# Second half of the first token chunk transposed by DMA instead of on TensorE, one PSUM bank per strip of the first half, and the small GELU and gate parameters loaded from ScalarE's queue

## The chip, the cores and the metric

The kernel runs on one core of a Trainium2 chip. The metric is the device time of one execution in microseconds (us). The profile's times count from the start of its span, which is about 1.8 us shorter than the device time of the same execution (218.6 against 220.37 us in the profiled run of the kernel before). The engines are called PE (TensorE; PEld is its weight load), ACT (ScalarE), DVE (VectorE), POOL (GpSimd) and SP (SyncE, which here only issues DMAs). "SPq" and "ACTq" in a trace line mean the queue of that engine while it issues a DMA.

## The reference, cut to what matters

Two branches over the same 2048 tokens of width 640 are mixed by a gate. Branch A is a state-space model: a complex linear recurrence along the tokens between two projections. Branch B is an MLP, 640 to 1728 to 640, with GELU.

```python
x = A_x                                                   # (1, 2048, 640) bf16
g = _sigmoid((x * gate_w).sum(-1, keepdims=True))
a = _A_ref(x, A_Lambda_re, ..., A_log_dt, A_Dskip)        # h = Lam_bar*h + x@B_bar ; y = 2*Re(h@C) + x*D
b = _B_ref(x, B_w1, B_b1, B_w2, B_b2)                     # gelu(x@w1 + b1) @ w2 + b2
return g * a + (1 - g) * b
```

## The kernel before

The tokens go in four chunks of 512. The first matmuls of both branches (x@w1, x@B_bar) sum over the features of a token and here read them along the partitions, so every chunk is needed transposed (`xT`). Chunks 1 to 3 come transposed by DMA. Chunk 0 is on the path to the first useful matmul, so it is loaded as it lies, in two halves of 256 tokens, and transposed on TensorE; VectorE and ScalarE copy the result from PSUM. The first matmuls are FF1 (x@w1) of chunk 0: six output tiles held in six PSUM banks, first for the first token half, then for the second. Tiles 7 to 14 follow; then the state-space stage ("SSM", first weights `BT_re`), and from there PE runs without a break to the end.

```python
    load_xn(0, 0, H)                                     # first 256 tokens, as they lie (SP queue)
    nc.scalar.dma_start(out=prmA[0:KS, :], in_=A_log_dt...)      # three small loads, ACT queue
    ...
    for kd in range(KD):                                 # KD = 5
        nc.sync.dma_start(out=w1a[kd][:], in_=B_w1[kd * P:(kd + 1) * P, 0:cut1])    # tiles 1 to 6
    load_xn(0, H, TPC)                                   # second 256 tokens
    for kd in range(KD):
        nc.sync.dma_start(out=w1b[kd][:, 0:F - cut1], in_=B_w1[..., cut1:F])        # tiles 7 to 14
    ...
    nc.gpsimd.dma_start(out=prmB[...], in_=B_b1...)      # three small loads, POOL queue: b1, gate_w
    nc.sync.dma_start_transpose(out=BT_re[:], in_=A_B_re[:, :])
    ...
    pA = bank(BF16)                                      # 8 PSUM banks in all
    pT = bank(BF16)

    def strip(kd, h):                                    # four strips in one bank, the fifth in pA
        return pT[:, kd * HT:(kd + 1) * HT] if kd < 4 else pA[:, (h + 1) * HT:(h + 2) * HT]

    def transposes(h):                                   # ten PE transposes of 128x128
        ...
    def take(kd, h):
        dst = xT[0][:, kd, h * HT:(h + 1) * HT]
        if kd % 2 == 0:
            nc.vector.tensor_copy(out=dst, in_=strip(kd, h))
        else:
            nc.scalar.activation(out=dst, in_=strip(kd, h), func=ACT.Identity)
    ...
    banks = [bank() for _ in range(FA)]                  # FA = 6
    for kd in range(KD):
        if kd == KD - 1:                                 # second token half, before the last kd of the first
            transposes(1)
            for j in range(KD):
                take(j, 1)
        for kf in range(FA):
            ff1_mm(banks[kf], 0, kf, kd, 0, HT)
    nc.scalar.activation(out=FS[:, :, 0:HC], in_=red, func=ACT.Sin, scale=TWO_PI_M)   # SSM's rotation tables
    ...                                                  # more Sin, then:
    for kd in range(KD):
        for kf in range(FA):
            ff1_mm(banks[kf], 0, kf, kd, HT, CH)         # second token half
        if kd == 2:
            nc.tensor.transpose(pA[:, P:P + NB], prmB[:], ident[0:NB, 0:NB])          # b1, gate_w to columns
            ...
    for kf in range(FA):
        ff1_act(banks[kf], 0, kf)                        # GELU: frees the six banks
    ff1(0, FA)                                           # tiles 7 to 14
```

Of the kernel before, what the change touches and what calls it, by code (L numbers as in the profile page):

```python
# [11 lines left out]
ACT = mybir.ActivationFunctionType  # L12
BF16 = mybir.dt.bfloat16
# [3 lines left out]
P = 128  # L17
T = 2048
D = 640
F = 1728  # L20
CH = 512
NCH = T // CH
KD = D // P
KS = D // P
KF = (F + P - 1) // P
F_LAST = F - (KF - 1) * P
NT = T // P
TPC = CH // P
# [10 lines left out]
def kernel(  # L39
# [19 lines left out]
    nc = tc.nc  # L59
    x2d = A_x.flatten_outer_dims()  # L60
# [11 lines left out]
    def bank(dtype=F32):  # L72
        return ps.tile([P, CH * 4 // (4 if dtype == F32 else 2)], dtype, name="bank")
# [4 lines left out]
    xT = [const.tile([P, KD, CH], BF16, name=f"xT{c}") for c in range(NCH)]  # L78
# [9 lines left out]
    ident = const.tile([P, P], BF16, name="ident")  # L88
    prmA = const.tile([3 * KS, P], BF16, name="prmA")
    NB = KS + KF  # L90
    prmB = const.tile([NB, P], BF16, name="prmB")
# [10 lines left out]
    xn = [None] * NCH  # L102
# [7 lines left out]
    H = TPC // 2  # L110

    def load_xn(c, a0=0, a1=TPC):
        if a0 == 0:
            xn[c] = xnp.tile([P, TPC, D], BF16, name="xn")
        r0 = c * CH + a0 * P
        nc.sync.dma_start(out=xn[c][:, a0:a1, :], in_=x2d[r0:r0 + (a1 - a0) * P, :].rearrange("(a p) d -> p a d", p=P))
# [4 lines left out]
    nc.scalar.dma_start(out=prmA[2 * KS:3 * KS, :], in_=A_Lambda_re.rearrange("(j p) -> j p", p=P))  # L121
    for kd in range(KD):
        nc.sync.dma_start(out=w1a[kd][:], in_=B_w1[kd * P:(kd + 1) * P, 0:cut1])
    load_xn(0, H, TPC)
    for kd in range(KD):
        nc.sync.dma_start(out=w1b[kd][:, 0:F - cut1], in_=B_w1[kd * P:(kd + 1) * P, cut1:F])
    make_identity(nc, ident[:])
    HC = CH // 4
    tfi = work.tile([P, HC], I32, name="e")
    nc.gpsimd.iota(tfi[:], pattern=[[1, HC]], base=0, channel_multiplier=0)  # L130
    nc.gpsimd.memset(prmB[:], 0.0)
    nc.gpsimd.dma_start(out=prmB[KS:NB - 1, :], in_=B_b1[0:(KF - 1) * P].rearrange("(j p) -> j p", p=P))
    nc.gpsimd.dma_start(out=prmB[NB - 1:NB, 0:F_LAST], in_=B_b1[(KF - 1) * P:F].rearrange("(j p) -> j p", p=F_LAST))
    nc.gpsimd.dma_start(out=prmB[0:KS, :], in_=gate_w.rearrange("(j p) -> j p", p=P))
    nc.sync.dma_start_transpose(out=BT_re[:], in_=A_B_re[:, :])
    nc.sync.dma_start_transpose(out=BT_im[:], in_=A_B_im[:, :])
    nc.sync.dma_start_transpose(out=xT[1][:], in_=x2d[CH:2 * CH, :])
# [5 lines left out]
    nc.sync.dma_start(out=Dbc[:], in_=A_Dskip.rearrange("(o d) -> o d", o=1).to_broadcast([P, D]))  # L143
    nc.sync.dma_start_transpose(out=xT[2][:], in_=x2d[2 * CH:3 * CH, :])
    nc.sync.dma_start_transpose(out=xT[3][:], in_=x2d[3 * CH:4 * CH, :])
    load_xn(1)

    ctx.enter_context(tc.manual_schedule(engines={E.PE, E.DVE, E.Activation}))


    class Clock:
        pe = 5.2
        act = 13.0
        dve = 0.0

# [36 lines left out]
    for _ in range(2):  # L192
        nc.tensor.matmul(wps[:, 0:P], lhsT=warm[:, 0:P], rhs=warm[:, 0:P], start=True, stop=True)
    pA = bank(BF16)
    pT = bank(BF16)
    HT = H * P


    def strip(kd, h):
        return pT[:, kd * HT:(kd + 1) * HT] if kd < 4 else pA[:, (h + 1) * HT:(h + 2) * HT]  # L200

    def transposes(h):
        for kd in range(KD):
            o = strip(kd, h)
            for a in range(H):
                nc.tensor.transpose(o[:, a * P:(a + 1) * P], xn[0][:, h * H + a, kd * P:(kd + 1) * P], ident[:])  # L206

    def take(kd, h):
        dst = xT[0][:, kd, h * HT:(h + 1) * HT]
        if kd % 2 == 0:  # L210
            nc.vector.tensor_copy(out=dst, in_=strip(kd, h))  # L211
        else:
            nc.scalar.activation(out=dst, in_=strip(kd, h), func=ACT.Identity)  # L213

    transposes(0)
    nc.tensor.transpose(pA[:, 0:3 * KS], prmA[:], ident[0:3 * KS, 0:3 * KS])

    def col(name, dtype=F32, n=KS):
# [6 lines left out]
    thp_c = col("thp_c")  # L225
    r_c = col("r_c")
    for kd in range(KD):
        take(kd, 0)
    nc.vector.tensor_copy(out=colA[:], in_=pA[:, 0:3 * KS])
    nc.scalar.activation(out=dt16[:], in_=ldt_c, func=ACT.Exp)  # L230
    nc.vector.tensor_copy(out=dt32[:], in_=dt16[:])
# [43 lines left out]
    def ff1_mm(p, c, kf, kd, t0=0, t1=CH):  # L275
        m = sizes[kf]
        w = w1a[kd][:, kf * P:kf * P + m] if kf < FA else w1b[kd][:, (kf - FA) * P:(kf - FA) * P + m]
        nc.tensor.matmul(p[:m, t0:t1], lhsT=w, rhs=xT[c][:, kd, t0:t1], start=(kd == 0), stop=(kd == KD - 1))  # L278
        pe(t1 - t0)
# [25 lines left out]
    gel_tile(0)  # L305
    banks = [bank() for _ in range(FA)]
    for kd in range(KD):
        if kd == KD - 1:
            transposes(1)
            for j in range(KD):  # L310
                take(j, 1)
        for kf in range(FA):
            ff1_mm(banks[kf], 0, kf, kd, 0, HT)
    nc.scalar.activation(out=FS[:, :, 0:HC], in_=red, func=ACT.Sin, scale=TWO_PI_M)  # L314
# [287 lines left out]
```

## Time and profile before

| | kernel before |
|---|---|
| device time, median of 6 runs | 220.63 us (220.2 to 220.8) |
| PE busy | 213.6 us, 98% of the span |
| PE busy from the SSM's first matmul to the kernel's last | 192.98 of 193.04 us |
| second half of FF1 starts | 9.79 us |
| first GELU starts | 15.29 us |
| first SSM matmul (timeline) | 22.50 us |

From the page of the kernel before: the span, and the shares of the chain of work that ended last, by engine.

```profile
span 218.6 us, 3401 instructions
...
PE 93%; ACT 3%; DVE 2%; issue 0%
```

The stretch table of the same trace. Columns: the stretch and its length in us, then the busy us of each engine (instructions in brackets), the granted TensorE clock, the mean DMA share and GB/s.

```profile
core 0: us, PE busy (x) PEld busy (x) DVE busy (x) ACT busy (x) POOL busy (x), PEclk, DMA share, GB/s
...
22.66:215.70 193.04, 192.98 (x1189) 115.68 (x1186) 174.10 (x348) 79.76 (x130) 1.03 (x2) 1.00 0.19 50
```

From 22.66 to 215.70 us PE is busy for 192.98 of 193.04 us. (The timeline starts the first SSM matmul at 22.50, when it enters PE; the stretch counts from 22.66, when the one before it ends.) Nothing that a change does to the loads at the start can shorten that; it can only let it begin earlier. So the question is what holds the head back. This is its timeline: start, duration, engine, line, operation, tiles, shapes, count, and in brackets idle time of the engine just before and what ended it.

```profile
3.96 0.38 SPq L116 DMA_DIRECT2D xn<-in_A_x_dram  x1
...
5.39 0.82 PE L278 MATMUL bank<-xT_76,w1a_80 128*128 128x256 bf16 x6 [0.16 <-DVE xT_76 L211]
...
8.38 0.73 PE L206 MATMUL bank<-ident,xn 128*128 128x128 bf16 x10 [0.20 <-DMA xn<-in_A_x_dram]
...
8.95 0.82 PE L278 MATMUL bank<-xT_76,w1a_84 128*128 128x256 bf16 x6
9.45 0.28 DVE L211 COPY xT_76<-bank 128x256 bf16<-128x256 bf16 x1
...
9.77 0.38 ACT L213 ACTIVATE xT_76<-bank 128x256 bf16<-128x256 bf16 x1 [2.52 <-DVE xT_76 L211]
9.79 0.81 PE L278 MATMUL bank<-xT_76,w1a_80 128*128 128x256 bf16 x6
...
10.19 0.49 DVE L211 COPY xT_76<-bank 128x256 bf16<-128x256 bf16 x2 [0.45 <-ACT xT_76 L213]
...
10.51 0.38 ACT L213 ACTIVATE xT_76<-bank 128x256 bf16<-128x256 bf16 x1 [0.36 <-DVE xT_76 L211]
...
10.91 1.28 ACT L314 ACT_TABLE_LOAD   x1
...
13.99 1.28 ACT L283 ACT_TABLE_LOAD   x1
...
15.22 0.38 PE L278 MATMUL bank<-xT_76,w1b_89 128*128 128x512 bf16 x1
...
15.29 8.14 ACT L283 ACTIVATE gel<-bank,colB 128x512 bf16<-128x512 f32 x14
...
16.03 0.38 PE L278 MATMUL bank<-xT_76,w1b_85 128*128 128x512 bf16 x1 [0.42 <-ACT gel L283]
...
22.50 1.24 PE L463 MATMUL bank<-xT_76,BT_re 128*128 128x512 bf16 x5
```

Four things are to be seen. FF1 of the first half starts at 5.39 after a wait for a copy. It is interrupted between 8.17 and 8.95: PE waits for the second token half (issued at 3.96) and spends 0.57 us on its transposes. The copies of that half go DVE, ACT, DVE, ACT, each starting where the other ends (only the fifth strip, which lies in the other bank, is copied beside the fourth), until 10.90; only then does ACT load its table for Sin (10.91), and so the table for GELU only at 13.99. The first GELU runs at 15.29, and since PE has used all its banks by then, the ninth FF1 tile waits: its first matmul starts at 16.03, 0.81 us after the last one, where such matmuls otherwise follow each other every 0.215 us.

### The profile page before, as it was taken

The numbers are of one execution on the slowest core, as the hardware profiler recorded it, in microseconds if no ns is written. First come the engines' busy times: TensorE is split into PE (matmuls) and PEld (weight loads), VectorE is DVE, ScalarE is ACT, GpSimd is POOL, SyncE is SP. The second block draws the span as 40 slices with busy tenths as digits, with TensorE's granted clock in tenths as the row PEclk, the third lists the DMA queues.
The fourth block names the chain that finished last, engine by engine and source line by source line (L and its number), as shares of the span: only waits on it lengthen the run. The fifth ranks groups of instructions, "written<-read, shape, count | busy, mean of one in ns | idle before, by whom it ended". The sixth has DMA issues, their size and how long they took to land.

```text
span 218.6 us, 3401 instructions
## 1 busy us (share of the span) xinstructions
PE 213.6 (98%) x1318; PEld 128.3 (59%) x1318; DVE 189.7 (87%) x396; ACT 94.6 (43%) x155; POOL 4.9 (2%) x15
## 2 busy tenths in 40 slices
PE   7999999999999999999999999999999999999994
PEld 4754444444577776444467777444457777777773
DVE  1779999999999999999999999999999999931153
ACT  2399756666597201556652200356663220022100
POOL 6001000000000000000000000000000000000000
PEclk9999999999999999999999999999999999999999
DMA  6999999910000025000000005100000000100011
GB/s 183 355 206 234 235 304 292 205 34 2 0 3 0 0 53 183 8 0 0 3 0 0 3 0 182 60 3 0 0 0 0 3 0 30 63 31 0 3 61 60
DMA packets 31072, 15.31 MB, mean 70 GB/s; under 512 B 23823, under 2 KB 31056, under 8 KB 31056
## 3 DMA queue, kind: packets, MB, share of 16 engines
q1 hardware_dynamic: 30786, 15.05, 26.8%
q8 instruction: 10, 0.16, 0.3%
q10 hardware_dynamic: 174, 0.04, 0.1%
q14 instruction: 6, 0.05, 0.1%
q0 software_dynamic: 96, 0.00, 0.0%
HBM read 7.22 MB, written 2.62 MB: 45 GB/s over the span
## 4 chain that ended last, share of the span: by engine, by line
PE 93%; ACT 3%; DVE 2%; issue 0%
PE bank L510 28%; PE bank L278 24%; PE bank L529 20%; PE bank L463 20%; PE bank L191 1%; ACT xT_76 L213 1%; ACT L283 1%; ACT L314 1%; DVE xT_76 L211 1%; PE bank L206 0%; DVE gel L261 0%; DVE gel L263 0%; ACT hs L316 0%; ACT gel L283 0%; DVE bu L262 0%
## 5 line engine op out<-in xcount | busy, mean ns | idle before, releaser
L510 PE MATMUL bank<-w_sb,gel 128*128 128x320 bf16 x448 | 61.6, 299 | 0.0
L510 PEld LDWEIGHTS <-gel 128*128 128x128 bf16 x448 | 43.7, 98 | 17.7
L283 ACT ACTIVATE gel<-bank,colB 128x512 bf16<-128x512 f32 (+1 forms) x56 | 37.0, 696 | 16.7 <-PE bank L278 16.7
L466 ACT ACTIVATE bu<-bank 128x512 bf16<-128x512 f32 x40 | 23.9, 597 | 39.7 <-PE bank L463 39.7
L529 PEld LDWEIGHTS <-hs 128*128 128x128 bf16 x330 | 31.8, 98 | 11.9
L419 DVE TENSOR_TENSOR_SCAN g<-r_c,carry,v 128x512 bf16<-128x512 f32 x30 | 37.1, 1272 | 0.0
L513 ACT ACTIVATE gb<-bank,gcol 128x320 f32<-128x320 f32 x32 | 16.5, 528 | 46.3 <-PE bank L510 34.0
L529 PE MATMUL bank<-CT_re,hs 128*128 128x320 bf16 (+2 forms) x165 | 27.1, 295 | 0.0
L529 PE MATMUL bank<-CT_im,hs 128*128 128x320 bf16 (+2 forms) x165 | 27.1, 295 | 0.0
L534 DVE SCALAR_TENSOR_TENSOR ot<-bank,gcol,gb 128x320 bf16<-128x320 f32 (+2 forms) x33 | 17.5, 536 | 8.6 <-PE bank L529 8.4
L496 DVE TENSOR_TENSOR bank<-xn,Dbc 128x320 f32<-128x320 bf16 (+2 forms) x33 | 14.4, 484 | 7.9 <-ACT gb L513 7.9
L463 PEld LDWEIGHTS <-BT_im 128*128 128x128 bf16 x100 | 9.8, 98 | 11.8
L463 PEld LDWEIGHTS <-BT_re 128*128 128x128 bf16 x100 | 9.8, 98 | 11.5
L400 DVE TENSOR_TENSOR v<-wa,wb 128x512 bf16<-128x512 bf16 x40 | 15.2, 422 | 0.6
L400 DVE TENSOR_TENSOR wa<-TCOS,g 128x1024 bf16<-128x1024 bf16 x20 | 13.7, 687 | 0.1
L400 DVE TENSOR_TENSOR wb<-TSIN,bu 128x1024 bf16<-128x1024 bf16 x20 | 13.7, 686 | 0.0
L400 DVE TENSOR_TENSOR wa<-TCOS,bu 128x1024 bf16<-128x1024 bf16 x20 | 13.7, 685 | 0.0
L400 DVE TENSOR_TENSOR wb<-TSIN,g 128x1024 bf16<-128x1024 bf16 x20 | 13.7, 685 | 0.0
L419 DVE TENSOR_TENSOR_SCAN g<-r_c,v 128x512 bf16<-128x512 f32 x10 | 11.8, 1211 | 0.0
L400 DVE TENSOR_TENSOR hs<-wa,wb 128x512 bf16<-128x512 bf16 x20 | 8.5, 425 | 0.6
L400 DVE TENSOR_TENSOR hs<-wb,wa 128x512 bf16<-128x512 bf16 x20 | 8.4, 419 | 0.0
L463 PE MATMUL bank<-xT_76,BT_re 128*128 128x512 bf16 x25 | 6.2, 379 | 0.0
(156 smaller groups left out, 250.4 us busy)
## 6 DMA issues: line engine op xcount, KB each, us to landing
out_dram<-ot SPq DMA_DIRECT2D x15, 160.0 KB, 1.8
w_sb<-in_B_w_dram SPq DMA_DIRECT2D x1, 2080.0 KB
xn<-in_A_x_dram SPq DMA_DIRECT2D x3, 640.0 KB, 4.2
xn<-in_A_x_dram SPq DMA_DIRECT2D x2, 320.0 KB, 3.8
gz<-zrow SPq DMA_DIRECT2D x16, 0.5 KB, 2.1
w1b_85<-in_B_w_dram SPq DMA_DIRECT2D x1, 240.0 KB
w1b_86<-in_B_w_dram SPq DMA_DIRECT2D x1, 240.0 KB, 4.6
w1b_87<-in_B_w_dram SPq DMA_DIRECT2D x1, 240.0 KB
```

The lines of the kernel that those rows point to most:

```text
L191: nc.tensor.matmul(wps[:], lhsT=warm[:, 0:P], rhs=warm[:], start=True, stop=True)
L278: nc.tensor.matmul(p[:m, t0:t1], lhsT=w, rhs=xT[c][:, kd, t0:t1], start=(kd == 0), stop=(kd == KD - 1))
L283: nc.scalar.activation(out=gel[c][:m, kf, :], in_=p[:m, :], func=ACT.Gelu_apprx_tanh, bias=b1_c[:m, kf:kf + 1])
L400: nc.vector.tensor_tensor(out=o, in0=a, in1=b, op=op)
L419: nc.vector.tensor_tensor_scan(s["g"][:, ri, :], r_c[:, ks:ks + 1].to_broadcast([P, CH]), s["v"][:, ri, :], init, ALU.mult, ALU.add)
L463: nc.tensor.matmul(p[:], lhsT=BT[:, kd, ks * P:(ks + 1) * P], rhs=xT[c][:, kd, :], start=(kd == 0), stop=(kd == KD - 1))
L466: nc.scalar.activation(out=bu[:, ri, :], in_=p[:], func=ACT.Identity)
L496: dve_now(ck.pe, 0.45, lambda: nc.vector.tensor_tensor(out=p[:, 0:d1 - d0], in0=xn[c][:, a, d0:d1], in1=Dbc[:, d0:d1], op=ALU.mult))
L510: nc.tensor.matmul(p[:, 0:d1 - d0], lhsT=gel[c][:m, kf, lo:lo + P], rhs=w2_sb[:m, kf, d0:d1], start=(kf == 0), stop=(kf == KF - 1))
L513: nc.scalar.activation(out=gb[:, d0:d1], in_=p[:, 0:d1 - d0], func=ACT.Identity, scale=gcol[:, 1, ti:ti + 1])
L529: nc.tensor.matmul(p[:, 0:d1 - d0], lhsT=hs[c][:, j, lo:lo + P], rhs=CT[:, j % KS, d0:d1], start=False, stop=(j == 2 * KS - 1), skip_group ...
L534: nc.vector.scalar_tensor_tensor(out=ot[:, d0:d1], in0=p[:, 0:d1 - d0], scalar=gcol[:, 0, ti:ti + 1], in1=gbs[ti][:, d0:d1], op0=ALU.mult, ...
```

## The change

Its intent: take the second token half off PE, DVE and ACT, let DVE and ACT copy the first half at the same time, and issue the small loads from ScalarE's queue instead of GpSimd's.

```diff
     for kd in range(KD):
         nc.sync.dma_start(out=w1a[kd][:], in_=B_w1[kd * P:(kd + 1) * P, 0:cut1])
-    load_xn(0, H, TPC)
+    nc.sync.dma_start_transpose(out=xT[0][:, :, H * P:CH], in_=x2d[H * P:CH, :])
     for kd in range(KD):
         nc.sync.dma_start(out=w1b[kd][:, 0:F - cut1], in_=B_w1[kd * P:(kd + 1) * P, cut1:F])
+    nc.gpsimd.memset(prmB[:], 0.0)
     make_identity(nc, ident[:])
...
-    nc.gpsimd.dma_start(out=prmB[KS:NB - 1, :], ...)      # and two more
+    nc.scalar.dma_start(out=prmB[KS:NB - 1, :], ...)      # and two more
...
+    load_xn(0, H, TPC)          # still needed as it lies, but first at about 69 us
     load_xn(1)
...
-        pe = 5.2                # the scheduling clock that orders DVE's later work
+        pe = 5.0
...
-    pT = bank(BF16)
+    pT = [bank(BF16) for _ in range(KD)]
...                              # strip(), transposes(), take() go; one transpose loop and one copy loop stay
     for kd in range(KD):
-        if kd == KD - 1:
-            transposes(1)
-            for j in range(KD):
-                take(j, 1)
         for kf in range(FA):
             ff1_mm(banks[kf], 0, kf, kd, 0, HT)
```

More of the change, by code (lines that the diff above doesn't have):

```diff
@@ L130 @@
     nc.gpsimd.iota(tfi[:], pattern=[[1, HC]], base=0, channel_multiplier=0)
-    nc.gpsimd.memset(prmB[:], 0.0)
-    nc.gpsimd.dma_start(out=prmB[KS:NB - 1, :], in_=B_b1[0:(KF - 1) * P].rearrange("(j p) -> j p", p=P))
-    nc.gpsimd.dma_start(out=prmB[NB - 1:NB, 0:F_LAST], in_=B_b1[(KF - 1) * P:F].rearrange("(j p) -> j p", p=F_LAST))
-    nc.gpsimd.dma_start(out=prmB[0:KS, :], in_=gate_w.rearrange("(j p) -> j p", p=P))
+    nc.scalar.dma_start(out=prmB[KS:NB - 1, :], in_=B_b1[0:(KF - 1) * P].rearrange("(j p) -> j p", p=P))
+    nc.scalar.dma_start(out=prmB[NB - 1:NB, 0:F_LAST], in_=B_b1[(KF - 1) * P:F].rearrange("(j p) -> j p", p=F_LAST))
+    nc.scalar.dma_start(out=prmB[0:KS, :], in_=gate_w.rearrange("(j p) -> j p", p=P))
     nc.sync.dma_start_transpose(out=BT_re[:], in_=A_B_re[:, :])
@@ L194 @@
     pA = bank(BF16)
-    pT = bank(BF16)
+    pT = [bank(BF16) for _ in range(KD)]
+    for kd in range(KD):
+        for a in range(H):
+            nc.tensor.transpose(pT[kd][:, a * P:(a + 1) * P], xn[0][:, a, kd * P:(kd + 1) * P], ident[:])
     HT = H * P
-    def strip(kd, h):
-        return pT[:, kd * HT:(kd + 1) * HT] if kd < 4 else pA[:, (h + 1) * HT:(h + 2) * HT]
-    def transposes(h):
-        for kd in range(KD):
-            o = strip(kd, h)
-            for a in range(H):
-                nc.tensor.transpose(o[:, a * P:(a + 1) * P], xn[0][:, h * H + a, kd * P:(kd + 1) * P], ident[:])
-    def take(kd, h):
-        dst = xT[0][:, kd, h * HT:(h + 1) * HT]
-        if kd % 2 == 0:
-            nc.vector.tensor_copy(out=dst, in_=strip(kd, h))
-        else:
-            nc.scalar.activation(out=dst, in_=strip(kd, h), func=ACT.Identity)
-    transposes(0)
     nc.tensor.transpose(pA[:, 0:3 * KS], prmA[:], ident[0:3 * KS, 0:3 * KS])
@@ L227 @@
     for kd in range(KD):
-        take(kd, 0)
+        dst = xT[0][:, kd, 0:HT]
+        if kd % 2 == 0:
+            nc.vector.tensor_copy(out=dst, in_=pT[kd][:, 0:HT])
+        else:
+            nc.scalar.activation(out=dst, in_=pT[kd][:, 0:HT], func=ACT.Identity)
     nc.vector.tensor_copy(out=colA[:], in_=pA[:, 0:3 * KS])
```

## The prediction

> **What bounds the kernel.** TensorE. The chain of waits is 93% PE; the stretch table has PE busy 192.98 of 193.04 us from 22.66 us (first SSM matmul, L463) to 215.7. The change touches only the first 22.66 us, where the timeline shows these losses: PE waits 0.16 us for the first xT copy (5.39); its first-half FF1 is broken at 8.17 by a 0.20 us wait for the second token half and ten PE transposes (8.38 to 8.95); DVE and ACT then copy that half in turns until 10.90, which holds the Sin table load back to 10.91, Sin to 12.21, the GELU table load to 13.99 and the first GELU to 15.29; so PE, out of PSUM banks, waits 0.42 us at 16.03 (0.7 us in schedule).
>
> **What the change removes.** Ten PE transposes (0.57 us of PE) and their six copies (1.45 us of serial DVE/ACT). With one bank per strip, ACT no longer alternates with DVE. The Trainium skill, "PSUM — Partial Sum Buffer", section on bank collisions, says two engines must not touch one bank x quadrant at once; the trace agrees: every ACT copy starts 0.02 us after a DVE copy ends.
>
> **What it adds or moves.**
> - A DMA transpose of 256x640. A traced 512x640 took 2.83 us of queue and 5.3 us to landing; at the ~290 GB/s seen during transposes, half the bytes save 1.1 us: about 4.2 us to landing (estimate). It issues later than the load it replaces (3.96): DMA semaphores are shared in turn, and with three more DMAs on the ScalarE queue w1a_84 now waits for w1a_80's landing (1.26+3.2=4.46), so the transpose issues near 4.95 and lands near 9.2 to 9.6.
> - w1b follows about 2 us later (last landing near 13.2; needed near 13.5): just in time. BT_re and BT_im land 1 to 1.5 us later (17 and 20; needed at 21.3 and 22.4): slack.
> - ACT issues three more DMAs; the gate_w one waits for xn's landing (3.9), so the first table load ends near 5.6, not 3.3, and the first ACT copy comes at 5.6 instead of 5.37. One bank and xT strip 1 wait for it: 0.2 to 0.3 us of PE, hidden by the wait for the DMA transpose. Moving small loads between queues gains nothing in itself, since they "will ultimately run on the same 16 DMA engines" (the Trainium skill, "DMA: Bandwidth & Descriptors", Issuing engines are not separate DMA queues).
> - On DVE the ten CT folds move a few instructions earlier in chunk 1; PE doesn't wait there.
>
> **Sum.** First-half FF1 ends near 8.6 (was 9.6); the second half starts when the transpose lands, near 9.4 (was 9.79): 0.4 us. Sin no longer waits for the copies; the GELU table load follows colB near 12, the first GELU starts near 13.3, and the 16.03 stall goes: 0.7 us. The SSM starts near 21.5 instead of 22.66, and the rest shifts unchanged: 1.1 us. Predicted 219.5 us, range 218.7 to 220.6. Faster by over 2%: 0.01; within 2%: 0.98; slower: 0.01.
>
> **What would show it.** The timeline: transpose issued 4.5 to 5.2; PE with one wait of 0.4 to 1 us on it; no wait at the ninth FF1 tile; first GELU at 13 to 13.8; first SSM matmul at 21.2 to 21.9; PE wholly busy afterwards.
>
> **What would make it wrong.** A first transpose that costs more than later ones (BT_re's queue time was 5.24 us, perhaps back-pressure): landing at 10.5 or later eats the gain, and w1b could stall PE. Landing below 8.7 would give up to 2 us.

## The result and the profile after

The changed kernel took 219.34 us (median of 6 runs, 218.79 to 219.76) against 220.63 us. The ratio is 0.9944 with a 95% interval of 0.9929 to 0.996; here and below a ratio is the mean time of one kernel's fast runs over the mean of the other's of the same rounds, so not quite the ratio of the medians. The gain of 1.3 us is clear of the noise. The kernel before was a little faster in all later groups of runs (220.37 or 220.38 us), so the gain is better put at 1.0 to 1.3 us.

The page after (line numbers are the changed kernel's):

```profile
span 217.0 us, 3363 instructions
...
PE 94%; DMA 3%; issue 0%; SPq 0%; DVE 0%
```

The stretch from the SSM's start on:

```profile
21.06:214.10 193.04, 192.45 (x1179) 115.64 (x1186) 173.26 (x345) 79.56 (x129) 1.03 (x2) 1.00 0.21 55
```

It is 193.04 us long, as before, and PE is busy in it for 192.45 us; the trace holds ten matmul records fewer there, so this is no sign of a new wait. The head after, in lines that answer to those shown of before:

```profile
3.69 0.33 SPq L123 DMA_DIRECT2D w1a_83<-in_B_w_dram  x1
...
3.98 1.28 ACT L217 ACT_TABLE_LOAD   x1 [3.98 <-DMA xn<-in_A_x_dram]
...
4.56 2.12 SPq L124 DMA_TRANSPOSE xT_76<-in_A_x_dram  x1
...
5.26 0.83 PE L267 MATMUL bank<-xT_76,w1a_80 128*128 128x256 bf16 x6
...
7.89 0.82 PE L267 MATMUL bank<-xT_76,w1a_84 128*128 128x256 bf16 x6
...
8.77 0.43 SPq L126 DMA_DIRECT2D w1b_89<-in_B_w_dram  x1
8.78 0.81 PE L267 MATMUL bank<-xT_76,w1a_80 128*128 128x256 bf16 x6
...
12.61 4.16 ACT L272 ACTIVATE gel<-bank,colB 128x512 bf16<-128x512 f32 x7
...
12.91 0.38 PE L267 MATMUL bank<-xT_76,w1b_88 128*128 128x512 bf16 x1
13.04 0.10 PEld L267 LDWEIGHTS <-w1b_89 128*128 128x128 bf16 x1 [0.24 <-DMA w1b_89<-in_B_w_dram]
...
13.13 0.38 PE L267 MATMUL bank<-xT_76,w1b_89 128*128 128x512 bf16 x1
...
20.90 1.24 PE L448 MATMUL bank<-xT_76,BT_re 128*128 128x512 bf16 x5
```

The transpose is issued at 4.56. FF1's first half now runs without a break from 5.26, and the second half starts at 8.78 instead of 9.79. The first GELU is at 12.61 instead of 15.29, and no FF1 tile waits for it. The line at 13.04 is new: the load of `w1b_89` arrives just as PE wants it. The SSM starts at 20.90 instead of 22.50: 1.0 us from the second half and 0.6 us from the stall that went. The chain of work that ended last (start, us, what) shows what the second half waited for:

```profile
4.56 4.17 DMA xT_76<-in_A_x_dram
...
8.78 2.12 PE bank L267 x18
```

The transpose took 4.17 us from issue to landing, and PE began 0.04 us later. What SP's own queue waited for in the first 30 us (engine and line, releaser, total us, times, longest):

```profile
SPq L123 <- DMA prmA<-in_A_Lambda_im_dram: 1.0, 1, 1.0
```

SP sat for 1.0 us ahead of the fourth `w1a` load, until a small parameter load from ACT's queue had landed. The program as built (its instruction list, not the source) shows why: the DMAs issued by SP and ACT take eight completion semaphores in turn, and a DMA that takes one again is made to wait until the last DMA on it has landed. With three more DMAs from ACT the fourth `w1a` load comes to wait for `A_Lambda_im`, the fifth for the first `w1a` load, and the transpose for `A_Lambda_re`.

### The profile page after: what moved, and what is told of

It reads as the page before. It is cut to its first block, busy times and chain, and to the rows that moved or that the text cites. A ratio compares the mean times of both kernels' runs of the same rounds, so it can differ in the third digit from the quotient of the medians.

```text
span 217.0 us, 3363 instructions
## 1 busy us (share of the span) xinstructions
PE 212.2 (98%) x1297; PEld 127.8 (59%) x1308; DVE 189.3 (87%) x393; ACT 94.1 (43%) x153; POOL 3.2 (1%) x12
## 3 DMA queue, kind: packets, MB, share of 16 engines
HBM read 7.22 MB, written 2.62 MB: 45 GB/s over the span
## 4 chain that ended last, share of the span: by engine, by line
PE 94%; DMA 3%; issue 0%; SPq 0%; DVE 0%
PE bank L495 28%; PE bank L267 26%; PE bank L514 20%; PE bank L448 20%; DMA xT_76<-in_A_x_dram 2%; DMA w1a_80<-in_B_w_dram 1%; SPq L116 0%; SPq L123 0%; DVE ot L519 0%; PE bank L313 0%
## 5 line engine op out<-in xcount | busy, mean ns | idle before, releaser
L481 DVE TENSOR_TENSOR bank<-xn,Dbc 128x320 f32<-128x320 bf16 (+2 forms) x33 | 14.5, 482 | 6.9 <-ACT gb L498 6.9
L448 PE MATMUL bank<-xT_76,BT_im 128*128 128x512 bf16 x25 | 6.2, 379 | 0.0
```

The source lines that it names most:

```text
L448: nc.tensor.matmul(p[:], lhsT=BT[:, kd, ks * P:(ks + 1) * P], rhs=xT[c][:, kd, :], start=(kd == 0), stop=(kd == KD - 1))
L481: dve_now(ck.pe, 0.45, lambda: nc.vector.tensor_tensor(out=p[:, 0:d1 - d0], in0=xn[c][:, a, d0:d1], in1=Dbc[:, d0:d1], op=ALU.mult))
```

## The experiments

The theory, D: the whole gain comes from the DMA transpose, about 1.0 us from the earlier second half of FF1 and 0.6 us from the GELU stall that vanishes with the copies. Rival B: one bank per strip gives a good part. Rival Q: moving the small loads gives a good part. Each run was timed in five rounds beside the kernel before, except the last.

One check holds for all of them. In each of the thirteen readable traces, the device time of the profiled execution less the start of its first SSM matmul lies between 197.75 and 198.02 us (before: 220.37 - 22.50 = 197.87; after: 218.79 - 20.90 = 197.89). So all differences arise in the head, and the folds that the changed scheduling clock moved on DVE cost nothing.

| run | median us | ratio to before (95%) | first SSM matmul in its trace |
|---|---|---|---|
| e1_control | 219.35 | 0.9952 (0.9927 to 0.9976) | 21.38 |
| e2_dma_only | 219.13 | 0.9932 (0.9908 to 0.9956) | 20.80 |
| e3_queue_only | 220.69 | 1.0005 (0.9979 to 1.0031) | 23.31 |
| e4_banks_only | 220.37 | 0.9987 (0.9963 to 1.0011) | 22.75 |
| e5_after_gpsimd | 218.70 | 0.9933 (0.9921 to 0.9945) | 21.34 |
| e6_after_packed | 219.59 | 0.9966 (0.9955 to 0.9978) | 21.31 |
| e7_before_dvecopies | 219.77 | 0.9975 (0.9962 to 0.9988) | not readable; e12: 22.01 |
| e8_after_delay4 | 220.66 | 1.0015 (1.0003 to 1.0027) | 22.62 |
| e9_after_w1bcols | 219.60 | 0.9961 (0.9949 to 0.9973) | 21.86 |
| e10_best1 | 218.96 | 0.9935 (0.9923 to 0.9947) | 21.14 |
| e11_best2 | 219.73 | 0.9972 (0.9959 to 0.9985) | 21.11 |

The kernel before had a median of 220.37 us in the first two groups (e1 to e4, e5 to e8) and 220.38 us in the third (e9 to e12). One of its eleven runs in the first group took 221.93 us, and the intervals of e1 to e4 are about twice as wide as the others. The median of e7 counts its slow execution (below); its ratio doesn't.

### e1_control: the changed kernel again

No edit.

> The changed kernel itself again, as a yardstick and for a second trace. Both theories: ratio to before 0.9944 (219.2 to 219.5 us); second half of FF1 starts between 8.6 and 9.2 us, when the DMA transpose lands; first SSM matmul between 21.0 and 21.5.

It took 219.35 us, as in the first measurement. Its trace has a second face of the same kernel: the SSM starts at 21.38, not 20.90, although the second half of FF1 runs as early (the parameter transpose in its midst is at 10.87 against 10.83). PE's weight loads between 12 and 14.5 us:

```profile
12.99 0.10 PEld L267 LDWEIGHTS <-w1b 128*128 128x128 bf16 x1 [0.37 <-DMA w1b<-in_B_w_dram]
13.60 0.98 PEld L267 LDWEIGHTS <-w1b 128*128 128x128 bf16 x6 [0.51 <-DMA w1b<-in_B_w_dram]
```

PE waits for the `w1b` loads. The matmuls of the seventh tile stand at 13.00 and 13.60 where the pitch is 0.215, so this wait cost 0.39 us (and one at the matmul before it 0.05 us). The changed kernel thus has a wait that comes and goes: it was absent in the first trace (the fastest of its runs, 218.79 us) and present in this one (219.26 us, near the median).

### e2_dma_only, e3_queue_only, e4_banks_only: one part of the change at a time

```diff
# e2: kernel before, with
-    load_xn(0, H, TPC)
+    nc.sync.dma_start_transpose(out=xT[0][:, :, H * P:CH], in_=x2d[H * P:CH, :])
...
+    load_xn(0, H, TPC)
     load_xn(1)
...
-        if kd == KD - 1:
-            transposes(1)
-            for j in range(KD):
-                take(j, 1)
```

> Only the DMA transpose; strips still share one PSUM bank and the small loads stay on the GpSimd queue. Theory D (the gain is the DMA transpose alone, half from the earlier second half of FF1, half from the vanished GELU stall): ratio 0.993 to 0.995, the transpose issued near 4.0, the second half of FF1 starts at 8.5 to 8.8, no stall at the ninth FF1 tile, first SSM matmul near 21.1. Rival B (one bank per strip gives half of it) or Q (the queue move gives half of it): ratio 0.997 or more.

```diff
# e3: kernel before, with
+    nc.gpsimd.memset(prmB[:], 0.0)      # ahead of make_identity
...
-    nc.gpsimd.dma_start(out=prmB[...], ...)    # three
+    nc.scalar.dma_start(out=prmB[...], ...)    # three
```

> Only the small loads moved to the ScalarE queue. Theory D: no gain, 0.1 to 0.6 us slower (ratio 1.000 to 1.003): the weight loads and the second token half wait for shared DMA semaphores, the second half's load issues near 4.6 instead of 3.96 and its PE transposes start near 8.9 instead of 8.38. Rival Q: faster by 0.5 us or more (ratio below 0.998).

```diff
# e4: kernel before, with
-    pT = bank(BF16)
+    pT = [bank(BF16) for _ in range(KD)]
+    pT2 = [None]
...
-        return pT[:, kd * HT:(kd + 1) * HT] if kd < 4 else pA[:, (h + 1) * HT:(h + 2) * HT]
+        if h == 0:
+            return pT[kd][:, 0:HT]
+        return pT2[0][:, kd * HT:(kd + 1) * HT] if kd < 4 else pA[:, (h + 1) * HT:(h + 2) * HT]
...
     banks = [bank() for _ in range(FA)]
+    pT2[0] = bank(BF16)
```

> Only one bank per strip for the first half; the second half is still transposed on TensorE and copied through two shared banks. Theory D: no gain (ratio 0.999 to 1.001): first FF1 matmul 0.15 us earlier, but the second half still waits for its load at 8.4 and the GELU stall stays. Rival B: faster by 0.5 us or more (ratio below 0.998).

The DMA transpose alone gives 0.9932, no less than the whole change; the queue move alone gives 1.0005 and the banks alone 0.9987, both with 1 inside the interval. That is what D expected, and e2 leaves nothing for the rivals to explain. The intervals of e3 and e4 alone, which reach down to 0.9979 and 0.9963, don't exclude a gain of 0.5 and 0.8 us. SP's queue and PE in e2 (SP lines first):

```profile
3.66 2.16 SPq L124 DMA_TRANSPOSE xT<-in_A_x_dram  x1
5.87 2.47 SPq L126 DMA_DIRECT2D w1b<-in_B_w_dram  x5
```

```profile
5.39 5.42 PE L279 MATMUL bank<-xT,w1a 128*128 128x256 bf16 x48
...
20.80 1.24 PE L460 MATMUL bank<-xT,BT_re 128*128 128x512 bf16 x5
```

The transpose is issued at 3.66, 0.9 us earlier than in the changed kernel, but lands only 0.1 us earlier, at 8.64: it takes 5.0 us, not 4.17. In e10, issued at 3.81, it also takes 5.0 us. So here an earlier issue hardly brought the landing forward. FF1's 48 first matmuls of 256 columns run in one piece of 5.42 us: PE waits at most 0.02 us for the transpose, and not for `w1b`. In e3 the second token half's load is issued at 4.60 instead of 3.96, and PE waits for it (PE lines):

```profile
9.60 0.73 PE L206 MATMUL bank<-ident,xn 128*128 128x128 bf16 x10 [0.98 <-DMA xn<-in_A_x_dram]
...
23.31 1.24 PE L463 MATMUL bank<-xT,BT_re 128*128 128x512 bf16 x5
```

The transposes start at 9.60 instead of 8.38, and the SSM at 23.31 instead of 22.50. The profiled execution took 221.1 us and the median 220.69, so the loss is there in the trace but not clear of the noise in the timing. In e4 the first copies run in parallel (ACT's at 4.62 instead of 5.37), and no gain is seen. Its trace doesn't show why: eight of its first FF1 matmuls ran at half pace (see e6), so PE itself came to the second half's transposes only at 9.04, with no wait for the load, and the alternating copies and the GELU stall followed as before. The SSM starts at 22.75.

### e5_after_gpsimd and e6_after_packed: undo one part

```diff
# e5: changed kernel, with the three prmB loads on nc.gpsimd again
# e6: changed kernel, with
-    pT = [bank(BF16) for _ in range(KD)]
+    pT1 = bank(BF16)
+    pT = [pT1[:, kd * HT:(kd + 1) * HT] if kd < 4 else pA[:, HT:2 * HT] for kd in range(KD)]
```

> The changed kernel with the small loads back on the GpSimd queue. Theory D, sharpened by the DMA-only run: the queue move costs, because the weight loads then wait for shared DMA semaphores; so this is the fastest yet, ratio 0.992 to 0.994 (218.7 to 219.1 us), the DMA transpose issued near 3.7, the last w1b load issued near 8, no wait of TensorE on w1b, first SSM matmul near 20.9. Rival Q (the queue move helps): ratio 0.996 or more.

> The changed kernel with the first-half strips packed in one shared bank again (queue move kept). Theory D: as the changed kernel (ratio 0.994 to 0.996): first FF1 matmul 0.1 to 0.5 us later, but the second half starts when the transpose lands, near 8.7 to 9.0, all the same. Rival B: ratio 0.997 or more.

e5 is the fastest median, 218.70 us. Its interval still overlaps that of the changed kernel (0.9929 to 0.996), and the two were not run in the same group, so "the queue move costs something" is likely and not shown by the timing alone. Part of the expectation failed: its trace does wait for `w1b`, 0.64 us over two matmuls (starts 12.49, 12.90 and 13.56, where the pitch is 0.215), and the SSM starts at 21.34. That execution took 219.18 us. The five runs lie in two clusters, 219.18 and 219.11 against 218.65, 218.62 and 218.70; 21.34 - 0.64 + 197.86 gives 218.56 us (an estimate for this execution without the wait), which is near the fast cluster.

e6 came out at 0.9966, between what the two theories had named (to 0.996 and from 0.997), with an interval that reaches into both. In its trace the first half starts at 5.39 (changed kernel: 5.26) and three steps between its matmuls are 0.21 us, not 0.11; a weight load also waits 0.4 us for `w1b`, which costs PE 0.07 us (matmuls at 13.25 and 13.53).

The Trainium skill, "TensorE: Matmul & The Clock Gate", section on the HAM clock gate, says that the array starts at half its clock and is released after a busy window whose phase is free-running, so that the moment varies from run to run. This agrees: the warm-up matmuls of 512 columns take 0.43 us each where later ones take 0.215, and slow steps at the start of FF1 are there in e4 (eight), e3, e6 and e10 (three each) and e1 (one) but not in the first trace of either kernel, so they are no part of the difference between those two. The clock record in the traces (the table `clock` of trace.npz) begins, at full clock, 4.9 us after the span's start in the kernel before, 5.1 in the changed kernel, 5.8 in e1, 6.2 in e10, 6.3 in e6, 6.4 in e3 and 7.2 in e4, which is where the slow steps end. For the time before it there is no record.

What one bank per strip is worth is best read from e2 (shared bank, 0.9932) against e5 (own banks, 0.9933), both without the queue move: nothing that can be seen. Whether it is worth something together with the queue move (e6 against the changed kernel, 219.59 against 219.34 us, intervals that overlap) stays open.

### e7_before_dvecopies and e12: the stall taken away by itself

```diff
# kernel before, with
-        if kd % 2 == 0:
+        if kd % 2 == 0 or h == 1:       # all second-half copies on DVE
             nc.vector.tensor_copy(out=dst, in_=strip(kd, h))
```

> The kernel before with all five second-half copies on VectorE, so that ScalarE loads the Sin table at 7.3 and need not wait for the copies. It keeps the TensorE transposes, and the second half of FF1 stays at 9.8. Theory D counts 0.5 to 0.7 us for the vanished GELU stall by itself: first GELU near 13.9 instead of 15.3, no wait at the ninth FF1 tile, ratio 0.9965 to 0.998. Rival: the stall is not worth its 0.4 us on the timeline because something else binds at once: ratio 0.999 or more.

> The kernel before with all second-half copies on VectorE once more, for its trace only: the profiled execution of the earlier run came out at 1290 us and can't be read. Theory D as stated there: first GELU near 13.9, no wait at the ninth FF1 tile, first SSM matmul 0.5 to 0.7 us earlier than in the kernel before (near 22.0).

The timed runs gave 0.9975, inside the expected range: the stall by itself is worth 0.5 to 0.6 us (0.3 to 0.8 by the interval). The profiled execution of e7 took 1290 us and is left out (see the last section). e12, one look, took 219.89 us. Its PE and its ACT:

```profile
8.66 0.73 PE L206 MATMUL bank<-ident,xn 128*128 128x128 bf16 x10 [0.54 <-DMA xn<-in_A_x_dram]
...
22.01 1.24 PE L463 MATMUL bank<-xT,BT_re 128*128 128x512 bf16 x5
```

```profile
7.22 1.28 ACT L314 ACT_TABLE_LOAD   x1
...
13.80 7.05 ACT L283 ACTIVATE gel<-bank,colB 128x512 bf16<-128x512 f32 x12
```

The transposes are still on PE and even start later than before (8.66), yet ACT's Sin table load moves from 10.91 to 7.22, the first GELU from 15.29 to 13.80, the ninth tile doesn't wait, and the SSM starts at 22.01, 0.49 us earlier. It is a one-line change that yields over a third of the gain without any DMA transpose.

### e8_after_delay4: the stall put back

```diff
# changed kernel, ahead of the GELU table load
+    idle = fwork.tile([P, D], F32, name="gb")
+    for _ in range(4):
+        nc.scalar.activation(out=idle[:]..., in_=red, func=ACT.Sin, scale=TWO_PI_M)
```

> The changed kernel with four spare Sin activations (about 3.3 us of ScalarE, into a scratch tile) ahead of the GELU table load. Theory D: the GELU stall comes back: first GELU near 15.9 instead of 12.6, TensorE waits about 2 us at the ninth FF1 tile, where it has 1.3 us of slack in the changed kernel; 1.5 to 2.3 us slower than the changed kernel (ratio 1.001 to 1.006 to the kernel before). Rival (ScalarE's start doesn't matter to the total): ratio 0.994 to 0.996.

The first GELU moved from 12.61 to 15.41 and the time to 220.66 us, 1.3 us above the changed kernel's 219.35. The ratio is within the expectation, the loss a little under it. The waits of PE (line, releaser, total us, times, longest):

```profile
PE bank L267 <- ACT gel L272: 0.6, 1, 0.6
PE bank L267 <- DMA xT<-in_A_x_dram: 0.4, 1, 0.4
PE bank L267 <- DMA w1b<-in_B_w_dram: 0.4, 1, 0.4
```

The GELU stall is back, but with 0.6 us of wait instead of 2: in this trace PE had already waited 0.4 us each for the transpose and for `w1b`, which took up part of the delay, and four activations took 3.0 us, not 3.3. The head has little slack left in any of its three supplies.

### e9_after_w1bcols, e10_best1, e11_best2: tries for a better version

e9 loads `w1b` in two column cuts, so that the seventh to ninth tile's weights come first. e10 adds the small loads on the GpSimd queue (as in e5). e11 adds a split first token load.

```diff
# e9 and e10
-    w1b = [const.tile([P, n1b], BF16, ...) for kd in range(KD)]
+    w1b_all = const.tile([P, KD, n1b], BF16, name="w1b")
+    w1b = [w1b_all[:, kd, :] for kd in range(KD)]
...
-    for kd in range(KD):
-        nc.sync.dma_start(out=w1b[kd][:, 0:F - cut1], ...)
+    for f0, f1 in ((cut1, cut1 + 3 * P), (cut1 + 3 * P, F)):
+        nc.sync.dma_start(out=w1b_all[:, :, f0 - cut1:f1 - cut1], in_=w1v[:, :, f0:f1])
# e11 also
-    load_xn(0, 0, H)
+    load_xn(0, 0, 1)
+    nc.scalar.dma_start(out=xn[0][:, 1:2, :], in_=x2d[P:2 * P, :]...)
-    for kd in range(KD):
-        for a in range(H):
+    for a in range(H):
+        for kd in range(KD):
             nc.tensor.transpose(pT...)
-    for _ in range(6):           # warm-up
+    for _ in range(5):
```

> The changed kernel with the second part of w1 loaded by two transfers cut by columns (what tiles 7 to 9 need first) instead of five cut by rows. In most runs of the changed kernel we think TensorE waits up to 0.5 us for the last w1b row block, which the DMA transpose pushed back. Theory W (that wait is what keeps the changed kernel at 219.3 rather than 218.8): 218.6 to 219.0 us, ratio 0.9925 to 0.994, no wait of TensorE on w1b in the profile, runs closer together. Rival (the spread has another cause): 219.3 as before, ratio 0.994 to 0.996.

> Column-cut w1b and the small loads back on the GpSimd queue. Theory W: 218.4 to 218.8 us (ratio 0.991 to 0.993) with no run near 219.2; first SSM matmul near 20.8 to 20.9. Rival: runs still split between 218.6 and 219.2.

> The same with the first token half loaded in two parts (one on each hardware queue), transposed part by part, and one warm-up matmul fewer. If the arrival of the first tokens now bounds the head: first FF1 matmul at 4.6 to 4.9 instead of 5.3, second half at 8.2 to 8.5, 0.1 to 0.4 us faster than the run before it (218.1 to 218.5). If the DMA transpose's landing bounds it: no change (218.5 to 218.8).

All three missed. e9 was 219.60 us, no faster than the changed kernel, and its trace says that the edit brought in a wait of its own (PE):

```profile
14.31 7.71 PE L269 MATMUL bank<-xT,w1b 128*128 128x512 bf16 x35 [0.56 <-DVE w1b L318]
```

`w1b` is now one tile. DVE writes the gate's column into it, behind the second of the two loads, which landed at 13.87; the eighth FF1 tile reads that tile and waits for DVE. So e9 is no test of the theory it was meant for. e10's trace has no wait on `w1b`, but its first FF1 matmuls were slow ones (see e6), and at 218.96 us it is not faster than e5. e11 has the same wait on DVE and a second one (PE):

```profile
5.27 0.16 PE L204 MATMUL bank<-ident,prmA 15*128 15x15 bf16 x1 [0.29 <-DMA prmA<-in_A_Lambda_re_dram]
```

The three small loads now stand behind half of the token load on ACT's queue, and the transpose of their values sits in PE's order ahead of FF1, which therefore starts at 5.37. Nothing is learnt from it about the arrival of the tokens.

## Why the prediction was right

The time was right, 219.34 us measured for 219.5 predicted, and so were the two causes, the earlier second half and the stall that goes. The sizes were less so: the first trace gives 1.0 + 0.6 us where 0.4 + 0.7 was booked, and a wait that was not booked took part of it back. That the total came out so close is therefore in part luck. Point by point:

- **Only the head can change: right.** The rest is 197.86 us within 0.2 us in all traces.
- **The GELU stall goes: right.** It was booked at 0.7 us; the trace gives 0.6, taking it away by itself (e7, e12) 0.5 to 0.6, and putting it back (e8) brought the time up again.
- **The copies, not the transposes on PE, held ACT back: right,** shown by e12, where the transposes stay and the stall goes.
- **The queue move gains nothing, and nothing is booked for the bank split: no gain of either was seen** (e3, e4, e2 against e5; for the banks with the open end named at e6). That the small loads make the big ones wait for semaphores was right in kind: SP waited 1.0 us.
- **The landing of the transpose: the right sum with a wrong term.** Issue to landing was put at 4.2 us and took 4.17; since it took 5.0 us in e2 and e10, where it was issued earlier, this closeness is luck in part. But the issue was put at 4.95 and came at 4.56, mostly because `w1a_80` landed 2.9 us after its issue, not 3.2; and a margin was added to the landing, to 9.4 from the 9.15 that the sum gives. So the second half of FF1 started 1.0 us earlier than before, not 0.4, after a wait of 0.23 us, not 0.4 to 1. The first GELU came at 12.61 where 13 to 13.8 was stated, for the same reason, and the first SSM matmul at 20.90 (21.38 in e1) where 21.2 to 21.9 was.
- **`w1b` "just in time": too optimistic.** PE waited for it not at all in one trace of the changed kernel and 0.44 us in the other. This took back most of what the former point gave, so the total of 1.1 us came out nearly right with two errors of opposite sign: 1.0 + 0.6 in the first trace (1.60 us), less 0.44 for `w1b` and 0.04 for a second half that starts later in the other (1.12 us). How often the wait occurs is open: only traced executions show it (by the steps between matmuls, in the other four traces with these loads behind the DMA transpose: none in e2, 0.07 us in e6, 0.57 in e8, 0.64 in e5), and the experiment meant to remove it (e9) brought in another.
- **First ACT copy at 5.6 and a short PE wait for it: wrong by 0.3 us.** The table load was over at 5.26 and the copy at 5.28; no wait of PE followed.
- **Two slips that change nothing:** the second half has five copies, not six, and ACT's copies start 0.03 us, not 0.02, after DVE's.

## What to carry to other kernels

When PE is busy without a break after the head, look only at what the head's end waits for. Moving a transpose off the compute engines paid here in two ways: the matmuls behind it started 1.0 us earlier, and the copies behind it no longer held up another engine's table loads (0.6 us). Reassigning those copies alone gave over a third of the gain. A small load moved to a hardware queue is not free where the queues share completion semaphores: look at what the big loads then wait for.

## What the Trainium skill lacked or had wrong

- "Advanced Engine Details and Errata", section X-Bar Transpose (TRN2), says transpose DMAs are as fast as regular ones and expects 350 to 400 GB/s. Here the transposes, of rows of 1280 bytes, ran at 288 to 291 GB/s where they were steady, with dips between them, against 353 to 404 GB/s for the plain `w2` load after them. This is the kernel before between 16 and 36 us, in 40 slices of 0.5 us, GB/s:

```profile
GB/s 289 291 289 289 139 168 251 288 291 229 138 194 232 288 291 290 197 159 73 208 291 289 289 290 117 118 230 310 404 397 374 384 384 366 369 366 361 353 221 234
```

- "DMA: Bandwidth & Descriptors" doesn't say how long a DMA transpose of a given size holds the issuing queue on this chip; it has only 631 cycles per instruction for small tiles, for "previous generations". Here it was held for 1.67 to 2.16 us for 256x640 (2.83 us for 512x640 in the kernel before), against about 0.45 us for a plain load. In e2, where SP issued without a wait, the first `w1b` load came 2.2 us after the transpose.
- "ScalarE: Activation LUTs", section What ACT_TABLE_LOAD costs, counts 1283 ns for the load and 1380 ns for a drain at each switch. The load took 1.28 us here; no drain can be seen: the last Sin ended at 13.98, the load began at 13.99, and the GELU began at 15.29, 0.02 us after it.
- No page has the very slow executions seen here (the nearest, "TensorE: Matmul & The Clock Gate", has a clock gate stuck at a quarter for over 50 us): one of e7's five (1290 us) and one of the kernel before's eleven in the third group (804 us). In e7's trace PE alone was slow, from its first matmul to its last. A line of that execution's chain:

```profile
109.29 66.05 PE bank L463 x50
```

  50 matmuls of 512 columns in 66.05 us are 1.32 us each, six times the usual 0.216; ACT's table load took its usual 1.28 us. The result file says a granted clock of 1.0, but this trace has no clock record at all, where each of the other thirteen has one that begins 4.8 to 7.2 us after the span's start; so the 1.0 is not a measurement. The cause is open.
